# A recurrent attention kernel on one core: reordering the end of each step, a new value projection, and weight loads in four pieces

## The chip, the core and the metric

The kernel runs on one core of one Trainium2 chip. The metric is the device time of one execution in microseconds (us), where lower is better. Executions of one kernel agree within about 0.3%.

## The reference, cut to what matters

Four layers are applied to a sequence of 2048 rows of 640 values, alternating between a block A and a block B, and each with a layer norm ahead of it and a residual behind it.

```python
def A(x, mem0, Wq, Wk, Wv, Wo, seg_len):      # 32 heads of 192, seg_len 32, 8 memory rows
    mem = mem0
    for s in range(S // seg_len):             # 64 segments, one after the other
        h = concat([mem, x[s]])               # 40 rows
        q, k, v = h @ Wq, h @ Wk, h @ Wv
        p = softmax(where(mask, q @ k.T * scale, -1e9))
        o = (p @ v) @ Wo
        mem = o[:8]                           # the next segment needs this
        out[s] = o[8:]
def B(x, wqkv, wo):                           # 32 heads of 20; each row attends to 8 rows, 2 apart
    ...
x = x + A(layernorm(x)); x = x + B(layernorm(x)); x = x + A(layernorm(x)); x = x + B(layernorm(x))
```

Block A is a recurrence: a segment's memory rows come out of the last matmuls of the segment before. Work of the next segment that needs `h` cannot begin earlier.

## The kernel before

Both A layers are computed in one loop of 66 steps and a short last one. In step t, layer 1 works on segment t and layer 3 on segment t - 2, side by side in one tile of 80 columns. Block B of the segments of step t - 1 is threaded through step t. Of A's weights (32 units of 960 KB, by kind k, q, v, o and head group 0 to 7), the kernel keeps 16 units in the on-chip memory, and loads the other 16 again in each step through a ring of 4 buffers.

The loading of a unit, and the order of a step (cuts are marked with `...`):

```python
    def unit(self, kind, i):
        if (kind, i) in self.units:
            return self.units[(kind, i)]
        ...
        self.nc.sync.dma_start(out=t_[:], in_=self.wA[self.place[(kind, i)]])
        ...

    def a_o(self, i):                      # output projection of head group i, into one accumulator
        ...
        for m in range(6):
            for c in range(NC):
                nc.tensor.matmul(self.acc[...], lhsT=w[:, m, P * c:P * (c + 1)], rhs=ot[:, m, self.cs], ...)

    def b_v(self, b):                      # values of block B: h2T is stationary, 320 columns move
        for par in range(2):
            ps = self.big("ps_bv")
            e0 = 2 * D + par * (D // 2)
            for c in range(NC):
                nc.tensor.matmul(ps[:, 0:D // 2], lhsT=self.h2T[:, c, :], rhs=self.wqkv[:, c, e0:e0 + D // 2], ...)
            ...                            # one copy on VectorE, one on ScalarE

    def step(self, t):
        ...
        for i in range(NQUAD):             # head groups 0 to 7
            last = i == NQUAD - 1
            if a:
                self.a_k(i, t)             # keys, queries
                self.a_q(i, t)
                if last:
                    self.a_pv(i - 1)       # softmax sums and p @ v of the group before
                elif i >= 2:
                    self.a_o(i - 2)
                self.a_v(i, t, 0)          # values, two halves
                if last:
                    self.a_s(i)            # scores, exp, mask
                self.a_v(i, t, 1)
                if 1 <= i and not last:
                    self.a_pv(i - 1)
            ...
                if i == 6:
                    self.b_ot()            # transpose of B's output, evicted on ScalarE to OTB
            if a and not last:
                self.a_s(i)
            if b is not None and i == 6:
                self.b_wo(b)               # B's output projection, reads OTB
            ...
        if nt < T:
            self.ln1(nt)                   # layer norm of the next step's rows
            self.ln1_apply(nt)
        if a:
            self.a_pv(7)
            self.a_o(5)
            self.a_o(6)
            self.a_o(7)
            if nt < T:
                self.mem_out(t)            # memory rows to hT, which the next step waits for
            self.b_x1(t)
```

In `a_pv`, two activations on ScalarE make the reciprocal R of the softmax sums, and three VectorE multiplications write OT: first the row blocks 0, 2, 3, 5, then the two halves of the row blocks 1 and 4. Each engine works through its instructions in the order of the program.

The names of tiles that recur below: hT holds h, the memory rows and the normed rows of the step, transposed; QT and Vt are the copies of queries and values that VectorE and ScalarE make of TensorE's results; Em is the masked exponential of the scores; OT is A's and OTB is B's output ahead of its output projection. A name that begins with `ps_` is a result of TensorE, such as `ps_d`, the softmax sums, or `ps_by`, B's output projection.

The softmax here doesn't subtract the row's maximum and nothing guards it: scores larger than these inputs give would overflow.

Of the kernel before, what the change touches and what calls it, by code (L numbers as in the profile page):

```python
# [10 lines left out]
BF16 = mybir.dt.bfloat16  # L11
# [6 lines left out]
P = 128  # L18
D = 640
NC = 5  # L20
DH = 192
NQUAD = 8
# [38 lines left out]
class Kernel:  # L61
    def __init__(self, ctx, tc, xT, m0T, wA, wqkv, wo, out):
        self.tc = tc
        self.nc = tc.nc
        self.x = xT
        self.mem0 = m0T
        self.wA = wA
        self.b_src = (wqkv, wo)
        self.out = out
        self.n_seg = 4 * xT.shape[0]  # L70
        pool = lambda name, bufs, **kw: ctx.enter_context(tc.tile_pool(name=name, bufs=bufs, **kw))
        self.cp = pool("consts", 1)
        self.wres = pool("wres", 1)
        self.wring = pool("wring", RING)
        self.ap2 = pool("act2", 2)
        self.ap3 = pool("act3", 3)
        self.bp = pool("bact", 1)
        self.xp = pool("xio", 1)
        self.ps_big = pool("ps_big", 4, space=PSUM)
        self.ps_one = pool("ps_one", 1, space=PSUM)  # L80
        self.units = {}
        self.place = {u: n for n, u in enumerate(unit_order())}
        self.resident = resident_units()
        self.build_consts()

    def build_consts(self):
# [24 lines left out]
        self.x1 = pers("x1", [P, NC, NX], 2)  # L111
        self.h2T = pers("h2T", [P, NC, P], 1)[0]
        self.KB = pers("KB", [P, NBC, P], 1)[0]
        self.VB = pers("VB", [P, BH // 2, 2 * BD + 1], 1)[0]
        nc.vector.memset(self.VB[:, :, BD:BD + 1], 1.0)
        self.On = pers("On", [P, 3 * P], 1)[0]
        self.YT = pers("YT", [P, NC, P], 1, zero=False)[0]
# [55 lines left out]
    def unit(self, kind, i):  # L173
        if (kind, i) in self.units:
            return self.units[(kind, i)]
        res = (kind, i) in self.resident
        if res:
            t_ = self.wres.tile([P, 3840], BF16, name=f"w_{kind}{i}")
        else:
            t_ = self.wring.tile([P, 3840], BF16, name="w_ring")  # L180
        self.nc.sync.dma_start(out=t_[:], in_=self.wA[self.place[(kind, i)]])
        v = t_[:].rearrange("p (a b) -> p a b", a=6 if kind == "o" else NC)
        if res:
            self.units[(kind, i)] = v
        return v

    def big(self, name):
# [92 lines left out]
        nc.vector.tensor_tensor(out=ot[64:P, :, 1, cs], in0=ov[64:P, :, 1, cs], in1=r[64:P, :, 1, cs], op=ALU.mult)  # L280
        self.ots[i] = ot

    def a_o(self, i):
        nc = self.nc
        w = self.unit("o", i)
        ot = self.ots.pop(i)[:].rearrange("p a b n -> p (a b) n")
        if i == 0:
            self.acc = self.one("acc")
        for m in range(6):
            for c in range(NC):  # L290
                nc.tensor.matmul(self.acc[:, NT * c + self.cs.start:NT * c + self.cs.stop], lhsT=w[:, m, P * c:P * (c + 1)], rhs=ot[:, m, self.cs],  # L291
                                 start=(i == 0 and m == 0 and c == 0), stop=(i == NQUAD - 1 and m == 5), skip_group_check=True)

    def lanes(self, flat):
        return flat.rearrange("p (c l n) -> p c l n", c=NC, l=2)
# [22 lines left out]
                nc.tensor.matmul(ps[:, NX * j:NX * (j + 1)], lhsT=self.ones[:], rhs=src[:, c, :], start=(c == 0), stop=(c == NC - 1))  # L318
        return ps

    def ln_small(self, ps):
        nc = self.nc
        m = self.ap2.tile([P, NX], F32, name="ln_m")
        nc.vector.tensor_scalar(out=m[:], in0=ps[:, 0:NX], scalar1=1.0 / D, scalar2=None, op0=ALU.mult)
        v = self.bp.tile([P, NX], F32, name="ln_v")
        nc.vector.tensor_tensor(out=v[:], in0=m[:], in1=m[:], op=ALU.mult)
        nc.vector.scalar_tensor_tensor(out=v[:], in0=ps[:, NX:2 * NX], scalar=1.0 / D, in1=v[:], op0=ALU.mult, op1=ALU.subtract)
        nc.scalar.activation(out=v[:], in_=v[:], func=ACT.Ln, bias=self.eps_t[:])
        r = self.ap2.tile([P, NX], F32, name="ln_r")
        nc.scalar.activation(out=r[:], in_=v[:], func=ACT.Exp, scale=-0.5)  # L330
        return m, r
# [17 lines left out]
        self.bsq = self.ln_sq(x1)  # L349

    def b_ln(self, b):
        self.bmr = self.ln_small(self.ln_stats(self.x1[b % 2], self.bsq))

    def b_ln_apply(self, b):
        self.ln_big(self.x1[b % 2], self.bmr, self.h2T[:, :, 64 * (b % 2):64 * (b % 2) + NX].rearrange("p c (l n) -> p c l n", l=2))
# [21 lines left out]

    def b_v(self, b):
        nc = self.nc
        for par in range(2):  # L380
            ps = self.big("ps_bv")
            e0 = 2 * D + par * (D // 2)
            for c in range(NC):
                nc.tensor.matmul(ps[:, 0:D // 2], lhsT=self.h2T[:, c, :], rhs=self.wqkv[:, c, e0:e0 + D // 2],  # L384
                                 start=(c == 0), stop=(c == NC - 1))
            src = ps[:, 0:D // 2].rearrange("p (h d) -> p h d", d=BD)
            dst = self.VB[:, :, (BD + 1) * par:(BD + 1) * par + BD]
            if par == 0:
                nc.vector.tensor_copy(out=dst, in_=src)
            else:  # L390
                nc.scalar.copy(out=dst, in_=src)

    def b_qexp(self, g):
        nc = self.nc
# [25 lines left out]
    def b_pv(self):  # L420
        nc = self.nc
        W = 2 * BD + 1
        on = self.On[:, 0:D // 2].rearrange("p (h d) -> p h d", d=BD)
        for g in range(2):
            ps = self.big("ps_bo")
            pv = ps[:, 0:8 * W].rearrange("p (h w) -> p h w", w=W)
            for hh in range(8):
                h = 8 * g + hh
                nc.tensor.matmul(pv[:, hh, :], lhsT=self.eb[:, h, :, :].rearrange("p a n -> p (a n)"), rhs=self.VB[:, h, :], start=True, stop=True)
            r = self.ap2.tile([P, 8, 1], F32, name="rB")  # L430
            nc.vector.reciprocal(out=r[:], in_=pv[:, :, BD:BD + 1])
            for par in range(2):
                rows = slice(64 * par, 64 * par + 64)
                d0 = (BD + 1) * par
                nc.vector.tensor_tensor(out=on[rows, 8 * g:8 * g + 8, :], in0=pv[rows, :, d0:d0 + BD],
                                        in1=r[rows].to_broadcast([64, 8, BD]), op=ALU.mult)
# [39 lines left out]
        self.asq = self.ln_sq(self.xin[t % 2])  # L476

    def ln1(self, t):
        self.amr = self.ln_small(self.ln_stats(self.xin[t % 2], self.asq))

    def ln1_apply(self, t):
        self.ln_big(self.xin[t % 2], self.amr, self.lanes(self.hT[t % 2][:, 0:NC * NT])[:, :, :, NM:LT])
# [1 line left out]
    def prologue(self):  # L484
        nc = self.nc
        self.xt, self.ots, self.qxs = {}, {}, {}
        self.x_load(0)
        nc.scalar.dma_start(out=self.m0T[:].rearrange("p c n -> p (c n)"), in_=self.mem0)
        self.x_take(0)
        nc.vector.tensor_copy(out=self.lanes(self.hT[0][:, 0:NC * NT])[:, :, 0, 0:NM], in_=self.m0T[:])  # L490
        self.ln1_sq(0)
        self.ln1(0)
        self.ln1_apply(0)

    def step(self, t):
# [3 lines left out]
        nt = t + 1  # L499
        if a:  # L500
            self.span_of(t)
        for i in range(NQUAD):
            last = i == NQUAD - 1
            if a:
                self.a_k(i, t)
                self.a_q(i, t)
                if last:
                    self.a_pv(i - 1)
                elif i >= 2:
                    self.a_o(i - 2)  # L510
                self.a_v(i, t, 0)
                if last:
                    self.a_s(i)
                self.a_v(i, t, 1)
                if 1 <= i and not last:
                    self.a_pv(i - 1)
            if b is not None:
                if i == 0:
                    self.b_ln(b)
                    self.b_ln_apply(b)  # L520
                if i == 1:
                    self.b_q(b)
                    self.b_qexp(0)
                    self.b_k(b)
                    self.b_qexp(1)
                if i == 2:
                    self.b_s(b, 0)
                    self.b_s(b, 1)
                    self.b_qexp(2)
                    self.b_v(b)  # L530
                if i == 3:
                    self.b_s(b, 2)
                    self.b_s(b, 3)
                if i == 4:
                    self.b_s(b, 4)
                    self.b_s(b, 5)
                if i == 5:
                    self.b_pv()
                if i == 6:
                    self.b_ot()  # L540
            if a and not last:
                self.a_s(i)
            if b is not None and i == 6:
                self.b_wo(b)
            if i == 2:
                yseg = t - 2 - LAG
                if yseg >= 0 and yseg % 4 == 3:
                    self.y_store(yseg // 4)
            if i == 5:
                if nt < self.n_seg:  # L550
                    self.x_take(nt)
                if nt % 4 == 3 and nt + 1 < self.n_seg:
                    self.x_load((nt + 1) // 4)
            if i == 6 and nt < T:
                self.ln1_sq(nt)
        if nt < T:
            self.ln1(nt)
            self.ln1_apply(nt)
        if a:
            self.a_pv(7)  # L560
            self.a_o(5)
            self.a_o(6)
            self.a_o(7)
            if nt < T:
# [61 lines left out]
```

## Time and profile before

| | before |
|---|---|
| time, median of 4 runs | 3559.98 us |
| busy share of TensorE, VectorE, ScalarE | 95%, 56%, 46% |
| DMA share of the weight queue, mean rate | 82.5%, 301 GB/s |
| a steady step, first key projection to first key projection | 53.25 us |
| of it matmuls back to back (53.25 less the four gaps read below) | 50.5 us |

These lines are from the page of the kernel before: the busy time of the engines (busy us, share of the span, instructions), the share of the weight queue in the time of 16 DMA engines, and the shares of the engines in the chain of work that ended last.

```profile
span 3560.6 us, 157110 instructions
...
PE 3365.6 (95%) x71346; PEld 2916.3 (82%) x71346; DVE 2007.0 (56%) x5692; ACT 1622.4 (46%) x4621; POOL 41.0 (1%) x150
...
q1 hardware_dynamic: 154656, 1057.33, 82.5%
...
PE 82%; DVE 7%; ACT 7%; issue 2%; DMA 2%; POOL 0%; POOLq 0%; SPq 0%; ACTq 0%
```

The chain is 82% TensorE, with 14% on VectorE and ScalarE: some of their work is on the path. A busy share of 95% hides this, because a matmul's end in the profile is a modelled one, about 0.17 us after its last column went in. Idle time must be read from starts. These are TensorE's lines of the timeline of one step's end (start, length, engine, line, operation, tiles, shape, count, and idle time before it with what ended it); the scores are left out.

```profile
start us, us, engine line op out<-in xcount [idle before <-releaser]
...
1036.45 0.34 PE L442 MATMUL ps_bt<-ident,On 128*128 128x128 bf16 x3
...
1037.95 1.04 PE L453 MATMUL ps_by<-OTB,wo_sb 128*128 128x64 bf16 x30 [0.89 <-ACT OTB L444]
1038.83 1.24 PE L206 MATMUL ps_k<-hT,w_ring 128*128 128x80 bf16 x30
1039.90 1.24 PE L206 MATMUL ps_q<-hT,w_q 128*128 128x80 bf16 x30
...
1041.40 0.98 PE L236 MATMUL ps_v<-w_ring,hT 128*128 128x384 bf16 x5
...
1042.50 0.98 PE L236 MATMUL ps_v<-w_ring,hT 128*128 128x384 bf16 x5
1043.32 0.31 PE L318 MATMUL ps_st<-xin,ones 128*128 128x64 bf16 x5
...
1044.33 0.30 PE L267 MATMUL ps_d<-Em,ones 80*128 80x320 bf16 x1 [0.56 <-DVE Em L258]
...
1045.83 1.24 PE L291 MATMUL ps_acc<-OT,w_ring 128*128 128x80 bf16 x30
1047.01 0.34 PE L291 MATMUL ps_acc<-OT,w_o 128*128 128x80 bf16 x5
1047.57 1.06 PE L291 MATMUL ps_acc<-OT,w_o 128*128 128x80 bf16 x25 [0.22 <-DVE OT L280]
1048.96 0.23 PE L206 MATMUL ps_k<-hT,w_ring 128*128 128x80 bf16 x2 [0.33 <-DVE hT L306]
```

Three readings show how starts are used.

- Thirty matmuls of 80 columns take 1.075 us from start to start (1038.83 to 1039.90), 35.8 ns each. The Trainium skill, "TensorE: Matmul & The Clock Gate", section "Back-to-back issue gap", gives N / 2.4 + 2.5 ns for an isolated matmul of N columns, which is 35.8 here. So nothing is waited for in this stretch, weight loads included.
- The five matmuls of 384 columns at 1042.50 fill 0.81 us, the ten short ones behind them 0.29. They end at 1043.61. The next instruction, `ps_d`, starts at 1044.33. The gap is 0.72 us, of which the profile shows 0.56 as idle.
- The last score matmul (not shown) starts at 1036.87 and `ps_by` at 1037.95. Less the 0.04 us of that matmul, this is a gap of 1.05 us.

ScalarE's lines of the same timeline show why `ps_by` waits: the transposes `ps_bt` are done at 1036.62, but OTB's copy stands behind a value copy and two activations.

```profile
start us, us, engine line op out<-in xcount [idle before <-releaser]
1036.22 0.47 ACT L243 CAST Vt<-ps_v 80x384 bf16<-80x384 f32 x1 [2.87 <-PE ps_v L236]
1036.60 0.43 ACT L275 ACTIVATE R<-ps_d 128x320 f32<-128x320 f32 x1
1037.07 0.47 ACT L276 ACTIVATE R<-R 128x320 f32<-128x320 f32 x1
1037.44 0.46 ACT L444 CAST OTB<-ps_bt 128x384 bf16<-128x384 f32 x1
```

### The profile page before, as it was taken

The page shows a single profiled execution, that of the slowest core. Times are in us where ns is not written, and L with a number is a line of the kernel's source. Part 1 is how long each engine was busy: PE and PEld are TensorE (multiplying, and loading weights), DVE is VectorE, ACT ScalarE, POOL GpSimd, SP SyncE. Part 2 cuts the span into 40 slices and gives each one's busy share as a digit, 9 for nine tenths or more (in the row PEclk, how much of TensorE's full clock was granted, in tenths as well). Part 3 has the DMA queues.
Part 4 walks back from the last instruction along what each step waited for, and adds up shares of the span by engine and source line. Part 5 has one row for each costly group of instructions (what it writes and reads, how often), then busy time and mean ns, then how long its engine had stood idle before and what let it go on. Part 6 is the DMA issues. An engine that isn't in the chain of part 4 may idle for free.

```text
span 3560.6 us, 157110 instructions
## 1 busy us (share of the span) xinstructions
PE 3365.6 (95%) x71346; PEld 2916.3 (82%) x71346; DVE 2007.0 (56%) x5692; ACT 1622.4 (46%) x4621; POOL 41.0 (1%) x150
## 2 busy tenths in 40 slices
PE   5899999999999999999999999999999999999998
PEld 4788888888888888888888888888888888888886
DVE  2455555555555555555555555555555555555554
ACT  1444444444444444444444444444444444444443
POOL 2000000000000000000000000000000000000000
PEclk8999999999999999999999999999999999999999
DMA  9988888888888888888888888888888888888886
GB/s 388 341 299 297 306 296 298 301 299 300 303 296 300 300 295 301 305 291 303 303 291 305 302 295 302 303 292 303 306 291 305 304 291 305 303 295 300 302 300 235
DMA packets 160077, 1072.63 MB, mean 301 GB/s; under 512 B 17840, under 2 KB 21936, under 8 KB 159280
## 3 DMA queue, kind: packets, MB, share of 16 engines
q1 hardware_dynamic: 154656, 1057.33, 82.5%
q8 instruction: 557, 9.13, 1.0%
q10 hardware_dynamic: 4752, 5.26, 0.4%
q14 instruction: 112, 0.92, 0.1%
HBM read 1059.89 MB, written 2.62 MB: 298 GB/s over the span
## 4 chain that ended last, share of the span: by engine, by line
PE 82%; DVE 7%; ACT 7%; issue 2%; DMA 2%; POOL 0%; POOLq 0%; SPq 0%; ACTq 0%
PE ps_v L236 21%; PE ps_k L206 16%; PE ps_q L206 16%; PE ps_acc L291 12%; PE ps_o L272 3%; PE ps_bv L384 3%; ACT R L275 2%; PE ps_by L453 2%; DVE OT L278 2%; ACT R L276 2%; PE ps_bq L364 2%; PE ps_bk L364 2%; PE ps_bs L408 2%; PE ps_s L253 2%; PE ps_s L254 2%
## 5 line engine op out<-in xcount | busy, mean ns | idle before, releaser
L243 ACT CAST Vt<-ps_v 80x384 bf16<-80x384 f32 x528 | 250.9, 475 | 1201.1 <-PE ps_v L236 1201.1
L236 PE MATMUL ps_v<-w_v,hT 128*128 128x384 bf16 x3960 | 715.5, 328 | 6.5 <-DMA w_v<-in_wA_dram 5.2
L236 PEld LDWEIGHTS <-hT 128*128 128x128 bf16 x5280 | 483.0, 99 | 277.4 <-issue 9.7
L278 DVE TENSOR_TENSOR OT<-ps_o,R 128x320 bf16<-128x320 f32 (+1 forms) x528 | 254.3, 482 | 676.8 <-ACT R L276 675.3
L206 PEld LDWEIGHTS <-w_ring 128*128 128x128 bf16 x15840 | 596.2, 100 | 42.1 <-issue 32.5
L206 PE MATMUL ps_k<-hT,w_ring 128*128 128x80 bf16 (+1 forms) x13860 | 565.4, 201 | 35.0 <-DVE hT L306 20.8
L206 PE MATMUL ps_q<-hT,w_q 128*128 128x80 bf16 (+1 forms) x13860 | 565.3, 201 | 2.7 <-DMA w_q<-in_wA_dram 2.2
L206 PEld LDWEIGHTS <-w_q 128*128 128x128 bf16 x13860 | 518.5, 100 | 3.0 <-DMA w_q<-in_wA_dram 2.4
L224 DVE CAST QT<-ps_q 128x480 bf16<-128x480 f32 (+1 forms) x528 | 339.3, 643 | 291.0 <-PE ps_q L206 284.6
L291 PE MATMUL ps_acc<-OT,w_ring 128*128 128x80 bf16 (+1 forms) x11880 | 485.2, 201 | 10.6 <-DMA w_ring<-in_wA_dram 6.0
L241 DVE CAST Vt<-ps_v 80x384 bf16<-80x384 f32 x528 | 291.8, 553 | 351.7 <-PE ps_v L236 349.4
L291 PEld LDWEIGHTS <-w_ring 128*128 128x128 bf16 x11880 | 444.3, 100 | 11.9 <-DMA w_ring<-in_wA_dram 6.5
L217 ACT CAST KF<-ps_k 128x320 bf16<-128x320 f32 (+1 forms) x528 | 219.2, 415 | 490.8 <-PE ps_k L206 490.8
L272 PEld LDWEIGHTS <-Vt 80*128 80x128 bf16 x4224 | 214.0, 98 | 88.8 <-issue 42.1
L236 PE MATMUL ps_v<-w_ring,hT 128*128 128x384 bf16 x1320 | 250.4, 329 | 1.2 <-DMA w_ring<-in_wA_dram 1.0
L276 ACT ACTIVATE R<-R 128x320 f32<-128x320 f32 (+1 forms) x528 | 243.9, 462 | 16.7
L256 ACT ACTIVATE E<-ps_s 80x320 bf16<-80x320 f32 (+1 forms) x528 | 221.1, 419 | 32.3 <-PE ps_s L254 32.3
L272 PE MATMUL ps_o<-Em,Vt 80*128 80x80 bf16 (+1 forms) x4224 | 234.6, 199 | 1.2 <-issue 0.8
L275 ACT ACTIVATE R<-ps_d 128x320 f32<-128x320 f32 (+1 forms) x528 | 224.6, 425 | 20.1 <-PE ps_d L267 20.1
L254 PE MATMUL ps_s<-QT,Kz 128*128 128x80 bf16 (+1 forms) x2112 | 216.3, 200 | 0.0
L253 PE MATMUL ps_s<-QT,KF 128*128 128x80 bf16 (+1 forms) x2112 | 216.0, 199 | 0.0
L267 PE MATMUL ps_d<-Em,ones 80*128 80x320 bf16 (+1 forms) x528 | 157.0, 297 | 35.0 <-DVE Em L258 34.9
(93 smaller groups left out, 3800.2 us busy)
## 6 DMA issues: line engine op xcount, KB each, us to landing
w_ring<-in_wA_dram SPq DMA_DIRECT2D x1056, 960.0 KB, 5.9
w_q<-in_wA_dram SPq DMA_DIRECT2D x7, 960.0 KB, 16.1
w_v<-in_wA_dram SPq DMA_DIRECT2D x6, 960.0 KB, 16.0
XT<-in_xT_dram ACTq DMA_DIRECT2D x16, 160.0 KB, 4.7
out_dram<-YT ACTq DMA_DIRECT2D x16, 160.0 KB, 3.0
wqkv_sb<-in_wqkv_dram SPq DMA_DIRECT2D x1, 2400.0 KB, 21.8
w_o<-in_wA_dram SPq DMA_DIRECT2D x2, 960.0 KB, 18.1
w_k<-in_wA_dram SPq DMA_DIRECT2D x1, 960.0 KB, 11.2
```

The source lines that it names most:

```text
L206: nc.tensor.matmul(ps[:, NT * n + c0:NT * n + c1], lhsT=w[:, c, P * n:P * (n + 1)], rhs=hT[:, NT * c + c0:NT * c + c1], start=(c == 0), st ...
L224: self.nc.vector.tensor_copy(out=qt[:, :, self.cs], in_=ps[:, 0:6 * NT].rearrange("p (a n) -> p a n", a=6)[:, :, self.cs])
L236: nc.tensor.matmul(ps[:, 0:384], lhsT=hT[:, NT * c:NT * c + P], rhs=w[:, c, 384 * pr:384 * (pr + 1)], start=(c == 0), stop=(c == NC - 1))
L241: nc.vector.tensor_copy(out=dst, in_=src)
L243: nc.scalar.copy(out=dst, in_=src)
L253: nc.tensor.matmul(sv[:, h, cs], lhsT=kf[:, NT * h:NT * h + P], rhs=qt[:, 3 * pr + 2 * j, cs], start=True, stop=False)
L254: nc.tensor.matmul(sv[:, h, cs], lhsT=kz[:, NT * h:NT * h + P], rhs=qt[:, 3 * pr + 1, cs], start=False, stop=True)
L272: nc.tensor.matmul(ov[:, pr, b, cs], lhsT=vt[0:NT, 512 * pr + w0:512 * pr + w0 + P], rhs=em[0:NT, 2 * pr + j, cs], start=st, stop=sp)
L275: nc.scalar.activation(out=rf, in_=dn, func=ACT.Ln)
L276: nc.scalar.activation(out=rf, in_=rf, func=ACT.Exp, scale=-1.0)
L278: nc.vector.tensor_tensor(out=ot[:, :, 0:3:2, cs], in0=ov[:, :, 0:3:2, cs], in1=r[:, :, :, cs], op=ALU.mult)
L291: nc.tensor.matmul(self.acc[:, NT * c + self.cs.start:NT * c + self.cs.stop], lhsT=w[:, m, P * c:P * (c + 1)], rhs=ot[:, m, self.cs], star ...
```

## The change

The intent is to keep TensorE fed. There are four parts:

1. The transpose of B's output goes ahead of the second half of value projection 6, so that OTB's copy is issued earlier and has more matmuls to hide behind.
2. The end of the step is reordered. Scores 7 go ahead of both halves of value projection 7; four of the six row blocks of output projection 5 go ahead of softmax-times-value 7; the row blocks 1 and 4, which OT gets last, are multiplied last; and the layer norm of the next step is cut in three parts that are placed among this.
3. B's values are projected like its queries, for the 64 new rows alone and in transposed form, then transposed on TensorE and copied.
4. Each load of a weight unit becomes four loads of a quarter, with rows of 1,920 B in place of 7,680 B.

```diff
-        self.nc.sync.dma_start(out=t_[:], in_=self.wA[self.place[(kind, i)]])
+        for h in range(4):
+            self.nc.sync.dma_start(out=t_[:, 960 * h:960 * (h + 1)], in_=self.wA[self.place[(kind, i)]][:, 960 * h:960 * (h + 1)])
...
-    def a_o(self, i):
+    def a_o(self, i, ms=(0, 2, 3, 5, 1, 4)):
...
-        for m in range(6):
+        for m in ms:
...
     def b_v(self, b):
...
-        for par in range(2):
-            ps = self.big("ps_bv")
-            e0 = 2 * D + par * (D // 2)
+        ps = self.big("ps_bv")
+        hs = slice(64 * (b % 2), 64 * (b % 2) + NX)
+        for n in range(NC):
             for c in range(NC):
-                nc.tensor.matmul(ps[:, 0:D // 2], lhsT=self.h2T[:, c, :], rhs=self.wqkv[:, c, e0:e0 + D // 2],
+                e0 = 2 * D + P * n
+                nc.tensor.matmul(ps[:, NX * n:NX * (n + 1)], lhsT=self.wqkv[:, c, e0:e0 + P], rhs=self.h2T[:, c, hs],
...
+    def b_vt(self, b):
+        ps = self.ps_big.tile([P, NC, P], BF16, name="ps_bvt", tag="big")
+        for n in range(NC):
+            nc.tensor.transpose(out=ps[:, n, :], in_=self.VTB[:, n, :], identity=self.ident[:])
...
     def step(self, t):
...
-        for i in range(NQUAD):
-            last = i == NQUAD - 1
+        for i in range(NQUAD - 1):
...
+            if b is not None and i == 6:
+                self.b_ot()
+            if a:
                 self.a_v(i, t, 1)
...
-            self.ln1(nt)
-            self.ln1_apply(nt)
+            self.ln1_sq(nt)
         if a:
+            self.a_k(7, t)
+            self.a_q(7, t)
+            if nt < T:
+                self.ln1(nt)
+            self.a_pv(6)
+            self.a_s(7)
+            if nt < T:
+                self.ln1_r()
+            self.a_v(7, t, 0)
+            self.a_v(7, t, 1)
+            self.a_o(5, (0, 2, 3, 5))
+            if nt < T:
+                self.ln1_apply(nt)
             self.a_pv(7)
-            self.a_o(5)
+            self.a_o(5, (1, 4))
             self.a_o(6)
             self.a_o(7)
```

## The prediction

> **What bounds the kernel.** The core runs 66 steps, in the timeline 53.26 us each when steady. TensorE sets it: the table of busy time gives it 95% (VectorE 56%, ScalarE 46%), the chain of waits 82%. Matmuls run back to back at 35.8 ns for 80 columns, 136 for 320, 55 for 128, 29 for 64, which agrees with N / 2.4 + 2.5 ns (Trainium skill, "TensorE: Matmul & The Clock Gate", Back-to-back issue gap): weight loads are not in the way. A step adds up to about 50.6 us of matmuls. The other 2.65 us are four gaps, by start-to-start times (the table of waits shows less: modelled ends):
>
> 1. 1.05 us before block B's output projection, waiting for OTB, queued on ScalarE behind a value eviction and two activations;
> 2. 0.71 us before the denominators of head group 7 (waiting for Em);
> 3. 0.39 us inside the last output projection (OT);
> 4. 0.50 us before the next step (accumulator to hT).
>
> DMA shows 82% busy, but loads move some 400 GB/s in bursts with idle time between; a ring buffer is free about 12 us before its next contents are needed, and a load lands in 5.9 us.
>
> **What the change does.**
> - The transpose of B's output goes ahead of the second half of value projection 6. Now 1.53 us of matmuls stand before its consumer: gap 1 closes, -1.05 us.
> - The tail: scores 7 move ahead of both value projections, two thirds of output projection 5 ahead of the last softmax-times-value, and the late rows of OT come last. In us after query projection 7: QT ready 0.9, but TensorE has only 0.72 of work, a new wait of 0.2; scores end 1.2, Em 3.0; the denominators would start at 3.55: gap 2 closes. R 4.85; OT's first part 5.36 against 5.41 for its consumer, the last 6.0 against 6.13: gap 3 closes, narrowly. Gap 4 stays. Net -0.85 us.
> - B's values: ten matmuls of 320 columns (1.36 us) become 25 of 64 (0.73) and five transposes of 128 (0.28): -0.35 us. VectorE's longer copy (+0.3 us, estimated) is off the path.
> - Each weight load becomes four with rows of 1,920 B. A 7,680 B packet takes 291 ns, one of 1,280 B 55: about 7 ns fixed, so four quarters take about 313. Two quarters start off a 256 B boundary, which costs extra beats (Trainium skill, "DMA: Bandwidth & Descriptors", How a descriptor splits into AXI transactions). Estimate: +8 to 10% DMA time. Neither this nor SyncE's 64 issues a step (0.33 us each) should reach TensorE, except in the DMA-bound first step (75.6 us), +3 us.
>
> **Sum.** 2.25 us of 53.26: a step of 51.0. Over 63 to 64 steps 142 us, less 3: 3560 - 139 = **3421 us**, range **3390 to 3470**. Chances: faster by over 2% 0.92, within 2% 0.07, slower 0.01.
>
> **What would show it.** Steps of 50.8 to 51.3 us; B's output projection without wait; at most 0.1 us on Em or OT at the end; a new 0.2 us on QT before scores 7; the hT wait still there; B's value matmuls near 1.0 us; DMA busy near 90%, no DMA waits after the first steps.
>
> **What would make it wrong.** Small descriptors limiting DMA, so that TensorE waits for ring weights; more semaphore waits stretching the 35.8 ns; VectorE late in the tail, tight to 0.1 us (0.3 us a step is 20 us); the longer copy delaying Em in the middle.

## The result

| | before | after |
|---|---|---|
| time, median | 3561.33 us (13 runs) | 3410.22 us (8 runs) |
| ratio | | 0.9577, 95% interval 0.9567 to 0.9586 |
| steady step | 53.25 us | 50.84 us |
| busy share of TensorE, VectorE, ScalarE | 95%, 56%, 46% | 97%, 59%, 48% |
| DMA share of the weight queue | 82.5% | 91.5% |

A ratio is the mean time of one kernel's fast runs over that of the other's of the same rounds, so it is not quite the ratio of the medians.

The page of the kernel after, with the lines that answer to those of before:

```profile
span 3410.2 us, 163092 instructions
...
PE 3323.2 (97%) x72666; PEld 2909.1 (85%) x72666; DVE 2007.4 (59%) x5693; ACT 1621.6 (48%) x4621; POOL 41.0 (1%) x150
...
q1 hardware_dynamic: 617760, 1057.53, 91.5%
...
PE 95%; DMA 3%; DVE 1%; issue 1%; POOL 0%; ACT 0%; SPq 0%; POOLq 0%
```

The chain is now 95% TensorE. VectorE and ScalarE have all but left it. TensorE's lines of the timeline at the same place of a step:

```profile
start us, us, engine line op out<-in xcount [idle before <-releaser]
...
1360.59 1.04 PE L470 MATMUL ps_by<-OTB,wo_sb 128*128 128x64 bf16 x30
...
1363.62 0.31 PE L324 MATMUL ps_st<-xin,ones 128*128 128x64 bf16 x5
...
1364.05 0.45 PE L278 MATMUL ps_o<-Em,Vt 80*128 80x80 bf16 x8
...
1364.81 1.79 PE L242 MATMUL ps_v<-w_ring,hT 128*128 128x384 bf16 x10
1366.44 0.88 PE L297 MATMUL ps_acc<-OT,w_o 128*128 128x80 bf16 x20
1367.15 0.30 PE L273 MATMUL ps_d<-Em,ones 80*128 80x320 bf16 x1
1367.30 0.45 PE L278 MATMUL ps_o<-Em,Vt 80*128 80x80 bf16 x8
1367.58 0.53 PE L297 MATMUL ps_acc<-OT,w_o 128*128 128x80 bf16 x10
1367.94 1.24 PE L297 MATMUL ps_acc<-OT,w_ring 128*128 128x80 bf16 x30
1369.02 1.24 PE L297 MATMUL ps_acc<-OT,w_o 128*128 128x80 bf16 x30
1370.59 0.41 PE L212 MATMUL ps_k<-hT,w_ring 128*128 128x80 bf16 x7 [0.33 <-DVE hT L312]
```

`ps_by` now follows its predecessor at the matmul rate, with no idle time before it (1.05 us before). `ps_d` of head group 7 (1367.15) starts where the 20 matmuls of output projection 5 end: 1366.44 + 20 x 0.0358 = 1367.16. In the last output projection the 30 matmuls run in one piece from 1369.02. The one wait of this list that the profile names in both kernels is the last line, for the memory rows in hT: 0.33 us shown, 0.50 between starts. And there is a new gap that the profile doesn't list as idle: the eight `ps_o` at 1364.05 need 0.28 us, but the scores behind them (left out here) start at 1364.53, 0.20 us late. They wait for QT, whose copy on VectorE ends at 1364.48:

```profile
1363.82 0.66 DVE L230 CAST QT<-ps_q 128x480 bf16<-128x480 f32 x1 [0.17 <-PE ps_q L212]
```

A step can be added up from starts: for each matmul the time to the start of the next, summed by what it writes, so that a gap counts to the matmul before it. One steady step of each kernel, worked out from the traces, in us:

| written | before | after | difference | what it is |
|---|---|---|---|---|
| keys, queries, values of A | 30.22 | 30.21 | 0 | at the array's rate in both |
| scores (64) | 3.32 | 2.27 | -1.05 | the gap ahead of B's output projection |
| layer norm sums (20) | 1.31 | 0.58 | -0.72 | the gap ahead of the softmax sums of group 7 |
| accumulator (240) | 9.58 | 9.10 | -0.49 | the gap for OT |
| softmax times value (64) | 2.25 | 2.45 | +0.20 | the new gap ahead of scores 7 |
| B's values | 1.36 | 1.00 | -0.35 | 10 matmuls of 320 to 25 of 64 (0.73) and 5 transposes (0.28) |
| all others | 5.22 | 5.22 | 0 | |
| sum | 53.25 | 50.84 | -2.41 | |

### The profile page after: what moved, and what is told of

The parts are those of the page before. It is cut to its first block, busy times and chain, and to the rows that moved or that the text cites. A ratio compares the mean times of both kernels' runs of the same rounds, so it can differ in the third digit from the quotient of the medians.

```text
span 3410.2 us, 163092 instructions
## 1 busy us (share of the span) xinstructions
PE 3323.2 (97%) x72666; PEld 2909.1 (85%) x72666; DVE 2007.4 (59%) x5693; ACT 1621.6 (48%) x4621; POOL 41.0 (1%) x150
## 3 DMA queue, kind: packets, MB, share of 16 engines
q1 hardware_dynamic: 617760, 1057.53, 91.5%
## 4 chain that ended last, share of the span: by engine, by line
PE 95%; DMA 3%; DVE 1%; issue 1%; POOL 0%; ACT 0%; SPq 0%; POOLq 0%
PE ps_v L242 25%; PE ps_k L212 16%; PE ps_q L212 16%; PE ps_acc L297 16%; PE ps_o L278 4%; PE ps_s L259 2%; PE ps_s L260 2%; PE ps_d L273 2%; PE ps_bq L375 2%; PE ps_bk L375 2%; PE ps_by L470 2%; PE ps_bs L425 2%; PE ps_bv L396 1%; PE ps_st L324 1%; DMA w_ring<-in_wA_dram 1%; PE ps_bo L446 1%
## 5 line engine op out<-in xcount | busy, mean ns | idle before, releaser
L242 PE MATMUL ps_v<-w_v,hT 128*128 128x384 bf16 x3960 | 727.0, 328 | 1.9 <-issue 0.8
L242 PE MATMUL ps_v<-w_ring,hT 128*128 128x384 bf16 x1320 | 239.6, 329 | 0.1
L297 PE MATMUL ps_acc<-OT,w_o 128*128 128x80 bf16 (+1 forms) x3960 | 173.5, 200 | 2.1 <-DMA w_o<-in_wA_dram 1.6
```

Of the source, the lines that this page charges most:

```text
L242: nc.tensor.matmul(ps[:, 0:384], lhsT=hT[:, NT * c:NT * c + P], rhs=w[:, c, 384 * pr:384 * (pr + 1)], start=(c == 0), stop=(c == NC - 1))
L297: nc.tensor.matmul(self.acc[:, NT * c + self.cs.start:NT * c + self.cs.stop], lhsT=w[:, m, P * c:P * (c + 1)], rhs=ot[:, m, self.cs], star ...
```

## The experiments

Twelve kernels were run; all computed the right result. The theory to test was: TensorE is the bound, and the gain is a sum of separate gaps closed plus matmul time saved, while cutting the loads is neutral. The main rival: the waits are one chain, or the earlier landing quarters are what made the gain.

### One part at a time

Each of these four is the kernel before with one part of the change. Their diffs are the corresponding parts of the diff above: for `only_ot`

```diff
+            if b is not None and i == 6:
+                self.b_ot()
+            if a:
                 self.a_v(i, t, 1)
...
-                if i == 6:
-                    self.b_ot()
```

for `only_tail` everything in `step` except that, with the new `a_o`; for `only_bv` the new `b_v`, `b_vt` and its call in head group 3; for `only_split` the four loads alone.

> The kernel before with one edit: the transpose of B's output goes ahead of the second half of value projection 6. My theory (the gains are separate gaps on TensorE that add up): the 1.05 us gap before B's output projection closes in each of 65 steps, so about -68 us, 3493 us, a step of 52.2 us, nothing else changed. Rival (the gaps are one serial chain, so closing one passes the wait on to the next): less than half of it, over 3525 us, with longer waits in the tail.

> The kernel before with the reordered tail alone (whole loads, old B values, old place of B's transpose). My theory, with the gaps as read from both traces (0.72 on Em and 0.49 on OT close, 0.20 on QT is new): -1.0 us a step, about -65 us, 3496 us. The blind prediction put it at -0.85 us a step, -54 us. Rival (the tail only works because B's eviction is out of the way, or because the loads land in quarters): under -40 us.

> The kernel before with the new value projection of B alone. My theory: TensorE is the bound, so the 0.35 us of matmul time that it saves in each step is gained in full: -23 us, 3538 us. Rival (VectorE's longer copy delays Em or QT in the middle of the step and gives it back): within 8 us of before, with new waits on VectorE.

> The kernel before with each weight load cut in four. My theory: no effect on the steady step of 53.26 us; the first, load-bound step is longer by about 5 us (80.8 against 75.6 in the trace of after): 3566 us; DMA share from 82% to about 88%. Rival (quarters that land earlier let TensorE start earlier, and this is where the 11 us beyond the prediction came from): faster than before by some 10 us, 3551 us.

| run | median | against before's 3560.78 | ratio, 95% interval | steady step |
|---|---|---|---|---|
| only_ot | 3497.38 us | -63.4 | 0.9820, 0.9806 to 0.9833 | 52.21 us |
| only_tail | 3499.26 us | -61.5 | 0.9825, 0.9810 to 0.9840 | 52.24 us |
| only_bv | 3540.61 us | -20.2 | 0.9940, 0.9927 to 0.9952 | 52.90 us |
| only_split | 3559.64 us | -1.1 | 0.9999, 0.9986 to 1.0011 | 53.25 us |

The four differences add up to -146.2 us, against -151.1 for the whole change. The steady steps add up more closely: -1.04, -1.01, -0.35 and 0.00 make -2.40 of -2.41 us. The gains are separate. The tables of waits show the same: with the transpose alone moved, the wait on OTB is gone and those on Em and OT stay; with the tail alone changed it is the reverse. From the waits of TensorE in `only_ot` (who waited for whom: us in total, times, longest):

```profile
PE ps_d L267 <- DVE Em L258: 35.0, 63, 0.6
PE ps_k L206 <- DVE hT L306: 20.8, 63, 0.3
...
PE ps_acc L291 <- DVE OT L280: 13.8, 62, 0.2
```

and in `only_tail`:

```profile
PE ps_by L462 <- ACT OTB L453: 57.7, 66, 0.9
PE ps_k L210 <- DVE hT L310: 20.8, 63, 0.3
```

`only_bv` gained 20 us of the 23 expected, and its step the full 0.35 us. VectorE's longer copy cost nothing. `only_split` didn't change the steady step. Both theories for it were off: its first two steps are 2.5 us longer (5 were expected) and the steps 2 to 63 together 2.8 us, but what follows them is 7 us shorter, so the time is the same. The shorter end is taken up below.

### Undoing one part of the change

`whole_load` is the changed kernel with one load for each unit again; `natural_rows` has the row blocks in the order 0 to 5; in `o5_after` no part of output projection 5 goes ahead.

```diff
# natural_rows
-    def a_o(self, i, ms=(0, 2, 3, 5, 1, 4)):
+    def a_o(self, i, ms=(0, 1, 2, 3, 4, 5)):
# o5_after
-            self.a_o(5, (0, 2, 3, 5))
...
-            self.a_o(5, (1, 4))
+            self.a_o(5)
```

> The changed kernel with the row blocks of the output projections taken in their natural order 0 to 5 again (projection 5 stays split as 0, 2, 3, 5 and 1, 4). My theory: OT's last parts are ready 0.6 us after its first; TensorE asks for row block 1 after 0.18 us instead of 0.72, so a wait of about 0.4 us inside the last output projection comes back: +26 us on 3410, 3436 us. Rival (the gap closed because softmax-times-value 7 comes earlier, and the order of rows adds nothing): within 6 us of 3410.

Measured: 3435.20 us, ratio to before 0.9650 (0.9635 to 0.9664), against 3410.22 with 0.9577. The steady step is 51.22 us, 0.38 more. TensorE's timeline of `natural_rows` shows the wait of before again, after five matmuls of the last output projection:

```profile
1428.36 0.34 PE L297 MATMUL ps_acc<-OT,w_o 128*128 128x80 bf16 x5
1428.92 1.06 PE L297 MATMUL ps_acc<-OT,w_o 128*128 128x80 bf16 x25 [0.21 <-DVE OT L286]
```

So the order of the row blocks is worth 25 us by itself. OT isn't finished earlier; it is read in the order in which it is written.

> The changed kernel with all of output projection 5 behind softmax-times-value 7, as it was before the change. My theory: the 0.72 us of its row blocks 0, 2, 3, 5 were what covered Em and the value eviction; without them TensorE waits 0.25 us for Em and 0.4 us for Vt: a step of 51.5 us, +44 us on 3410, 3454 us. Rival (moving scores 7 up was enough to close the gap on Em): within 0.2 us a step, under 3423 us.

Measured: 3455.55 us, ratio 0.9706 (0.9690 to 0.9722), a step of 51.54 us. Between starts, TensorE loses 0.24 us ahead of the softmax sums (waiting for Em) and 0.45 us ahead of softmax-times-value (waiting for Vt). Its timeline shows the second:

```profile
1433.04 0.30 PE L273 MATMUL ps_d<-Em,ones 80*128 80x320 bf16 x1
1433.63 0.46 PE L278 MATMUL ps_o<-Em,Vt 80*128 80x80 bf16 x8 [0.29 <-DVE Vt L247]
```

Moving scores 7 up was therefore not enough to close the gap on Em. The 20 matmuls that were moved with it are the cover: they cost nothing, since they have to be done anyway and their inputs have long been there.

> The changed kernel with each weight load whole again. My theory, now that the split alone moved the time by 1 us: within 8 us of the changed kernel's 3410 us, with a steady step of 50.84 us as there; the first two steps some 3 us shorter, the last three some 5 us longer; DMA share back from 91.5% to about 86%. Rival (at the faster step the loads have become tight and the quarters are needed): steady steps longer than 50.9 us, over 3430 us, with waits on ring weights.

Measured: 3419.63 us, ratio 0.9605 (0.9590 to 0.9619), which doesn't overlap with the changed kernel's 0.9567 to 0.9586; DMA share 84.8%. The steady step is 50.84 us, the same. Making the loads whole again cost 9 us, a little more than the 8 that the theory allowed. Stretches of the traces, worked out from starts, in us (step 64 and what follows it are the narrow steps at the end, in which only one of the two A layers has work):

| stretch | before | only_split | whole_load | after |
|---|---|---|---|---|
| steps 0 and 1 | 123.9 | 126.4 | 126.6 | 128.2 |
| steps 2 to 63 | 3303.7 | 3306.5 | 3160.3 | 3157.7 |
| step 64 | 46.6 | 44.1 | 46.6 | 43.1 |
| from step 65 to the last matmul | 63.3 | 58.8 | 62.8 | 58.2 |

The split pays at the end: 7 us in the kernel before and 8 us in the changed one. The other kept traces agree: from step 64 on, the five kernels with whole loads take 107.8 to 110.3 us, and the seven with four pieces 100.8 to 105.2.

The obvious reason would be that a narrow step needs less TensorE time for the same 16 units, and that TensorE can now begin on the first quarter of a unit. That isn't what made the gain here. For each of the 32 units from step 64 on, the first matmul started after the last quarter had landed, by at least 0.15 us in `only_split` and 0.30 us in `after`; in the kernel before, each unit had landed at least 0.83 us ahead. (It does happen in five other runs with pieces: 2 to 12 of the 32 units were begun up to 1.5 us before their last piece landed.) What shrinks are waits of TensorE for which the profile names no releaser. In all five traces looked at (those of the table and `rows960_one_issue`, below), every such wait of over 0.15 us in steps 2 to 63, 65 in number, ends 1.1 to 1.65 us after a packet of the queue that carries instructions (q8) has ended, where 9% of all moments lie so; these bounds were set after looking. From step 64 on, waits that end in this way sum to 7.1 us in `before` and 2.0 in `only_split`, to 9.4 in `whole_load` and 3.9 in `after`, so they are some 5 us of the 7 and of the 8. It looks as if TensorE waited for its own instructions there, and less so when the loads are cut. No run tests this; the cause stays open.

Mostly the same waits make some of the steps 2 to 63 uneven: 5 steps are over 0.05 us longer than the steady one in `before` (all 62 together 1.9 us), 13 in `after` (5.6 us), 20 in `whole_load` (8.2 us). The prediction expected no waits for loads after the first steps; the profile of `after` names 1.0 us of them, in three waits.

### How much splitting the loads can bear

> The changed kernel with each weight load in eight pieces of 960 B rows. Doubles the one cost of the split. With about 7 ns per packet, a row of a unit takes 8 x 43 = 344 ns of a DMA engine against 316 in quarters and 291 whole, and issues take 42 us of SyncE in a step of 51. My theory (quarters are free only because DMA has room left): the DMA share goes from 91.5% to 98% or more and TensorE begins to wait for ring weights, +30 to +150 us. Rival (row size doesn't matter to TensorE at this rate): a steady step still of 50.84 us, within 10 us of 3410 apart from a longer first step.

```diff
-        for h in range(4):
-            self.nc.sync.dma_start(out=t_[:, 960 * h:960 * (h + 1)], in_=self.wA[self.place[(kind, i)]][:, 960 * h:960 * (h + 1)])
+        for h in range(8):
+            self.nc.sync.dma_start(out=t_[:, 480 * h:480 * (h + 1)], in_=self.wA[self.place[(kind, i)]][:, 480 * h:480 * (h + 1)])
```

Measured: 4671.90 us, ratio 1.3136 (1.3111 to 1.3160). TensorE did begin to wait, but the time rose by 1262 us over the changed kernel in place of 30 to 150, and the DMA share didn't go up to 98%; it fell. From the page of `eighths`, the share of the weight queue and the chain:

```profile
q1 hardware_dynamic: 1235232, 1057.81, 79.6%
...
SPq 44%; PE 28%; DMA 22%; issue 5%; DVE 0%; ACT 0%; ACTq 0%
```

SPq, the sequencer that issues the loads, is the largest part of the chain. Its timeline in `eighths`:

```profile
1999.63 12.56 SPq L186 DMA_DIRECT2D w_ring<-in_wA_dram  x25
```

and in the changed kernel:

```profile
2000.27 12.09 SPq L186 DMA_DIRECT2D w_ring<-in_wA_dram  x17
```

In both, the queue is occupied without a break, but in the changed kernel part of this is waiting for ring buffers. Back to back, two issues start 0.474 us apart in both traces (the most frequent distance to within 1 ns, and the median in `eighths`). Sixty-four in a step are 30 us of 50.8; 128 are 61 us. My expectation had 42 us for the 128, because it took 0.33 us for each, which is how long the issue of a whole load lasts in the trace of before. (The mean granted clock of TensorE fell to 0.943 in `eighths`, against 0.992 in the changed kernel, so part of the extra time may be slower matmuls between waits.) My theory that DMA itself would run full had fallen. The new one was that the number of issues is the limit. The test keeps the short rows and takes away the issues: the weights are laid out in DRAM so that one load consists of eight pieces with rows of 960 B.

```diff
-        for h in range(4):
-            self.nc.sync.dma_start(out=t_[:, 960 * h:960 * (h + 1)], in_=self.wA[self.place[(kind, i)]][:, 960 * h:960 * (h + 1)])
+        self.nc.sync.dma_start(out=t_[:].rearrange("p (h c) -> p h c", h=8), in_=self.wA[self.place[(kind, i)]].rearrange("h p c -> p h c"))
...
+    wA = wA.reshape(N_UNITS, P, 8, 480).transpose(0, 2, 1, 3)
```

> The changed kernel with each weight load as one instruction again, but from a layout in which it consists of 960 B rows in DRAM, like the eighths; so the rows of the eighths with an eighth of their issues. Eighths took 4672 us with a DMA share of only 80%, so my theory for it (DMA itself runs full) has fallen. New theory: SyncE's issues, 0.474 us apart when they are back to back, and their waits bound the eighths; then this one runs near the changed kernel, 3400 to 3470 us, with a higher DMA share than the eighths, above 88%. Rival (960 B rows can't be moved fast enough whatever issues them): over 4000 us.

Measured: 3446.83 us, ratio 0.9681 (0.9667 to 0.9696), with the packets of 960 B taking 44 ns (median) in both kernels. From the page of `rows960_one_issue`:

```profile
q1 hardware_dynamic: 1115168, 1057.33, 98.7%
```

The same rows moved with a DMA share of 98.7%, and 35 of the steps 2 to 63 still took 50.84 us (to 0.05; in the changed kernel 49). So it was the separate issues, each with the waits that belong to it, and not the short rows. The spans of the profiled runs differ by 32 us from the changed kernel's; 11 of them lie in the first two steps (139.2 us against 128.2), 11 in steps 2 to 63 and 10 behind these. Of the step of `eighths`, some 69 us, the issues explain 61; what makes up the rest was not tested.

> The changed kernel with the four pieces cut at multiples of 256 B (rows of 1792, 2048, 1792 and 2048 B in place of 1920). If the quarters that started off a boundary cost extra beats, as the blind prediction assumed, the DMA share falls by about 1.5% of the span and the packets take 74 and 83 ns, 314 a row, or less. If alignment costs nothing here, the four packets again add up to 316 ns and the DMA share stays at 91.5% within 0.5. The time should be that of the changed kernel, 3410 us, in both cases.

```diff
-        for h in range(4):
-            self.nc.sync.dma_start(out=t_[:, 960 * h:960 * (h + 1)], in_=self.wA[self.place[(kind, i)]][:, 960 * h:960 * (h + 1)])
+        for c0, c1 in ((0, 896), (896, 1920), (1920, 2816), (2816, 3840)):
+            self.nc.sync.dma_start(out=t_[:, c0:c1], in_=self.wA[self.place[(kind, i)]][:, c0:c1])
```

Measured, in one run of unknown state: 3415.88 us, a steady step of 50.84 us, a DMA share of 91.4%, and packets of 74 and 84 ns, which is 316 for the four of a row. In the changed kernel the packets of 1,920 B take 79 ns in the median and in the lowest tenth, again 316. Alignment made no difference. The extra beats that the prediction assumed from the Trainium skill, "DMA: Bandwidth & Descriptors", section "How a descriptor splits into AXI transactions", don't show; the fixed cost of a packet, some 8 ns (79 x 4 - 291 = 25 for three packets more), is all that the split adds per row in the median.

### A version that beats both

The new gap of 0.20 us ahead of scores 7 can be covered in the way that the change itself uses: with a row block of output projection 5. `fill` does that. `fill_act` also moves the first value copy of head group 7 from VectorE to ScalarE.

```diff
             self.a_pv(6)
+            self.a_o(5, (0,))
             self.a_s(7)
...
-            self.a_o(5, (0, 2, 3, 5))
+            self.a_o(5, (2, 3, 5))
# fill_act alone, in a_v
-        if pr == 0:
+        if pr == 0 and i < 7:
             nc.vector.tensor_copy(out=dst, in_=src)
```

> The first edit of fill_act alone. In the trace of the changed kernel the value eviction on VectorE ends 0.09 us before softmax-times-value 7 reads it. My theory: with the row block moved up, TensorE reaches it 0.18 us earlier and waits there instead of for QT: a step of 50.8 us, 0.03 less than the changed kernel's 50.84, about 3408 us. Rival (that eviction is not on the path): 50.66 us as in fill_act.

> The changed kernel with two edits that should beat it: one row block (0) of output projection 5 goes ahead of scores 7, into the 0.20 us in which TensorE waits for QT, and the first value eviction of head group 7 goes from VectorE to ScalarE, which is idle then. My theory: the rest of the tail moves up by 0.18 us and nothing else binds: a step of 50.66 us, -11 us, 3399 us. Rival (R, on ScalarE, or OT is now what the last output projection waits for, since it was ready only 0.06 us ahead): a wait on OT takes its place, and the step stays within 0.05 us of 50.84.

`fill` (one run, state unknown, 3411.8 us) has a steady step of 50.83 us, 0.01 less than the changed kernel. The wait moved. TensorE's timeline of `fill`:

```profile
1416.98 0.30 PE L273 MATMUL ps_d<-Em,ones 80*128 80x320 bf16 x1
1417.28 0.46 PE L278 MATMUL ps_o<-Em,Vt 80*128 80x80 bf16 x8
```

and VectorE's:

```profile
1416.67 0.55 DVE L247 CAST Vt<-ps_v 80x384 bf16<-80x384 f32 x1
```

The softmax sums need 0.14 us, so `ps_o` could start at 1417.12. It starts at 1417.28, just after VectorE's value copy ends (1417.22). The table of waits doesn't name this, since the 0.16 us are hidden under the modelled end of `ps_d`. With that copy on ScalarE (`fill_act`) both are gone: 3397.97 us, ratio 0.9544 (0.9529 to 0.9558), a steady step of 50.66 us, 12 us less than the changed kernel. The timeline of `fill_act`:

```profile
1408.79 0.30 PE L273 MATMUL ps_d<-Em,ones 80*128 80x320 bf16 x1
1408.93 0.45 PE L278 MATMUL ps_o<-Em,Vt 80*128 80x80 bf16 x8
```

The only gap that is left in a step is the 0.50 us for the memory rows. I found no matmuls that could stand there, but no run tried any.

## Why the prediction was right

The prediction said 3421 us with a range of 3390 to 3470; the time is 3410.22. Point by point:

- *TensorE is the bound, at 35.8 ns for 80 columns, and four gaps are what can be gained.* Shown: after the change the sum of keys, queries and values is the same to 0.01 us, and each part of the change gained its own gap.
- *Gap 1 closes, -1.05 us.* Shown by `only_ot` (a step of 52.21 us, -1.04) and by the sum of the step.
- *Gap 2 closes, with a new wait of 0.2 us on QT.* Shown: -0.72 and +0.20 us. `o5_after` shows that the matmuls moved ahead of the softmax sums do it. The walk along the chain put the softmax sums at 3.55 us after query projection 7; in the trace it is 1367.15 - 1363.62 = 3.53.
- *Gap 3 closes, narrowly.* Shown, by `natural_rows` too. Its size was the term that was off: the prediction counted 0.39 us where the trace of before has 0.49, because OT's first part held TensorE up as well, by 0.11 us (1047.01 against 1045.83 + 30 x 0.0358 = 1046.90 in the timeline of before), and only the second wait, the one that the profile names, was read. This 0.10 us, and 0.06 in smaller terms, made a step of 50.84 us where 51.0 was predicted. The 11 us between the prediction and the time are not this alone. Steps 2 to 63 gained 146.0 us, where 62 times 2.25 makes 139.5: 10 us more for the shorter step, less 4 for uneven ones. The end gained 8.6 us where about 2.5 was left for it, by an effect that the prediction didn't have, and the first two steps lost 4.3 in place of 3. That the whole came so close is in part luck.
- *Gap 4 stays.* Shown: 0.33 us in both lists, 0.50 between starts.
- *B's values -0.35 us, VectorE's longer copy off the path.* Shown by `only_bv`: a step of 52.90 us, -0.35. The estimate of +0.3 us for the copy was too high: it takes 0.53 us for 640 elements of bf16, where the copy of 320 from fp32 took 0.49, so its rate nearly doubled (1.20 against 0.65 elements per ns). The type that it reads changed, but so did the layout of what it writes and the number of partitions (64 in place of 128), and no run separates these. An effect of the type would agree with the Trainium skill, "VectorE: DVE Perf Modes", section "Why PSUM operands drop a tier", by which an operand in PSUM allows at most a doubled rate, and fp32 none; the prediction had not looked it up.
- *The split loads cost 8 to 10% DMA time and +3 us in the first step, and nothing else.* The DMA time went from 82.5% of 3560.6 to 91.5% of 3410.2, which is +6% (the packets of a row went from 291 to 316 ns in the median, +8.6%); the first two steps became 4 us longer. What the prediction missed are the narrow steps at the end, where the split gains 7 to 8 us. It also had the issues too cheap: 0.33 us each, where pieces that follow each other start 0.474 us apart; at four pieces this didn't matter. Its reason for part of the cost, alignment, is not borne out by `aligned_quarters`.

Of its list of what could go wrong, "small descriptors limiting DMA" was the right place for a wrong reason. There is a limit close by, but it is the rate at which SyncE issues loads, and it is reached between four and eight pieces.

## What to carry to other kernels

Measure gaps on TensorE from start to start and put the largest pieces of independent matmul work in front of the latest operand; then read operands in the order in which they are written, which alone was worth 25 us here. Where the gaps are separate waits, as here, their sizes add up, and a prediction can be made by walking the chain with measured durations. When a load is cut into pieces, count the issues of the queue as well as the bytes: eight pieces, 128 issues of 0.474 us in a step of 51 us, cost 1262 us, while the same short rows under 16 issues cost 37.

## What the Trainium skill lacked or had wrong

- "TensorE: Matmul & The Clock Gate", "Back-to-back issue gap", gives about 81 ns for a matmul of 128 columns in a stream where each has its own weight load, and calls N / 2.4 + 2.5 ns the value of an isolated matmul. Here each matmul has its own weight load (71,346 of each), and the short formula holds in the stream: 35.8 ns at 80 columns, 29 at 64, and 55 at 128, the last only in runs of three to five transposes.
- "DMA: Bandwidth & Descriptors", "Issuing engines are not separate DMA queues", calls the sequencer's time to initiate a DMA usually small relative to the DMA itself. It isn't for pieces of 120 KB: issues from SyncE start 0.474 us apart when they follow each other, while 120 KB need about 0.32 us at the 388 GB/s of the first slice of before. The page does have a cost in another place, for "previous generations" in a table on trn3: 512 cycles for each copy instruction, which would be an estimated 0.43 us at the 1.2 GHz that "Trainium Kernel Development and Optimization", section "NeuronCore Architecture", gives for this engine. Most issues in the trace of `eighths` last 0.43 us, but those of whole loads in the trace of before last 0.33.
- "DMA: Bandwidth & Descriptors", "How a descriptor splits into AXI transactions": the extra beats of rows that start off a 256 B boundary were not seen; the packets of a row took 316 ns both ways.
- "Perfetto Trace Analysis", "DMA Optimizations", says that splitting DMAs into smaller sections may let the task complete sooner where the DMA engines are generally idle. They were not idle here (82.5%), so this doesn't contradict it: the steady step didn't change (53.25 and 53.25 us), and the 7 to 8 us gained at the end came without any matmul that began on a part of a unit (in `only_split` and `after`). The section doesn't give the cost of one more issue, 0.474 us here.
